# Local attention and a tanh-shrink MLP on one core: a new program with q, k, v cast in one GpSimd ring, bias by TensorE and a new planner

## The chip, the cores and the metric

The kernel runs on one core of a Trainium2 chip. The core has five engines, each with its own queue of instructions worked off in order: TensorE (PE: matmuls, with PEld its weight loads), VectorE (DVE), ScalarE (ACT), GpSimd (POOL) and SyncE (SP). Sixteen DMA engines move data between HBM and the on-chip memory SBUF; SP and POOL issue the transfers here. Matmul results go to PSUM, eight banks of 2 KB per partition. The metric is device time in microseconds of one execution, as the median of several runs.

## The reference

Sliding-window attention with eight global keys and a bias linear in distance, then a two-matrix MLP whose activation is `h - tanh(h)`:

```
q, k, v: (4, 8, 768, 64) f32    n_global, n_local = 8, 96    w_in: (512, 2048)  w_out: (2048, 512)

scores = q @ k.T / 8
rel = pos[:, None] - pos[None, :]
is_global = pos[None, :] < n_global
is_local = (rel >= 0) & (rel < n_local)
dist = where(is_global & ~is_local, n_local, abs(rel))
scores = where(is_global | is_local, scores - slopes * dist, -1e9)    # slopes = 2 ** -(h + 1)
a = softmax(scores)
x = (a @ v).transpose(0, 2, 1, 3).reshape(3072, 512)
h = x @ w_in
out = (h - tanh(h)) @ w_out                                           # (3072, 512) f32
```

## The kernel before

**Tiles.** The 4 x 768 positions are cut into 24 tiles of 128 (`NU`), six per batch (`NQ`), each with all eight heads. Because the window is 96 wide, a tile's queries need only two key blocks: the tile's own (`o = 0`) and the one before it (`o = 1`). The eight global keys and values are copied into the first columns of each previous block (`a_K`, `a_V`). The first tile of a batch has one block only.

**Stages of a tile `u`.** Three loads of 256 KB in f32 from SP (L143), each of 1,024 rows of 256 B; three casts to BF16, on POOL apart from q and k of tile 0 (L157, L160); a transpose of q and k, by PE for `u < 8` (`PE_T`, L169) with its eviction on ACT and DVE (L180, L182), else by a DMA transpose (L173); scores by PE, block by block (`a_S`, L190), each into a pair of PSUM banks; `exp` on ACT (L198); a multiply by a precomputed `exp(-slope * dist)` on DVE (`a_M`, L202); values by PE with a column of ones for the denominator (`a_AV`, L213, L217); the division on DVE (`a_R`, L225, L226); a transpose of x, by PE for `u < 9` (`PE_X`, L240, L249), else by DMA (L252).

**MLP.** The first product runs for one tile at a time for the first six tiles (`EARLY`) and for three together from there on (moving operands of 128 or 384 columns), 16 blocks of 128 hidden units with four matmuls each (`m1`, L273); `tanh` on ACT (L284) and the subtraction on DVE (L290) make g. The second product has 16 matmuls of 512 columns per tile (`m2`, L300), is copied out by ACT (L307) and stored by SP (L310).

**Loads and their order.** POOL issues the eight weight loads of 1 MB each, which are cast on the way (L149, L152). The list `before` gives the order: tiles 0 to 3, four of `w_in`, four of `w_out`, tiles 4 to 6, then the rest. From the third item on, an item after or among the weights waits for the landing of the item two places back (`gate_of`, `started`), so that two are in flight.

**Order on the engines.** All is written out by hand: `plan()` gives each operation an engine, a duration, what it comes after and which buffers it takes, and repeatedly picks the operation that can start first; the resulting list is the order on every queue (`manual_schedule`). `WARM = (1.4, 19.0)` fills PE's gaps up to 19 us of planned time with matmuls on zeros (L265). PSUM is two pools: two pairs of banks (`ps_big`) for scores and values, four single banks (`ps_one`) for the rest. The masks are made with iota on POOL, seven DVE operations on f32 and eight `exp` of 384 columns on ACT (L88 to L107).

Of the kernel before, what the change touches and what calls it, by code (L numbers as in the profile page):

```python
# [1 line left out]

# [10 lines left out]
ENG = mybir.EngineType  # L13


@with_exitstack
def kernel(
# [29 lines left out]
    NV = 8  # L47
    PE_T, PE_X = 8, 9
    HT = 3


    EARLY, EARLY2 = 6, 4
    groups = [[u] for u in range(EARLY)] + [[u, u + 1, u + 2] for u in range(EARLY, NU, HT)]
    group_of = {u: g for g, us in enumerate(groups) for u in us}

    cpool = ctx.enter_context(tc.tile_pool(name="const", bufs=1))
    stpool = ctx.enter_context(tc.tile_pool(name="stage", bufs=4))
    bpool = ctx.enter_context(tc.tile_pool(name="bpool", bufs=3))
    kpool = ctx.enter_context(tc.tile_pool(name="kpool", bufs=9))
    ppool = ctx.enter_context(tc.tile_pool(name="ppool", bufs=3))  # L60
    xpool = ctx.enter_context(tc.tile_pool(name="xpool", bufs=3))
    tpool = ctx.enter_context(tc.tile_pool(name="tpool", bufs=4))
    hpool = ctx.enter_context(tc.tile_pool(name="hpool", bufs=3))
    gpool = ctx.enter_context(tc.tile_pool(name="gpool", bufs=3))
    opool = ctx.enter_context(tc.tile_pool(name="opool", bufs=4))

    ps_big = ctx.enter_context(tc.tile_pool(name="ps_big", bufs=2, space=bass.MemoryType.PSUM))
    ps_one = ctx.enter_context(tc.tile_pool(name="ps_one", bufs=4, space=bass.MemoryType.PSUM))

    ident = cpool.tile([P, P], BF16, name="ident")  # L70
    mk = cpool.tile([P, H, 3, P], BF16, name="mk")
    rmat = cpool.tile([P, 3, P], FP32, name="rmat")
    tmp01 = cpool.tile([P, 2, 2, P], FP32, name="tmp01")
    zero = cpool.tile([P, 512], BF16, name="zero")
    w_in_bf = [cpool.tile([P, CD, DFF // WJ], BF16, name=f"w_in_bf{j}") for j in range(WJ)]
    w_out_bf = [cpool.tile([P, FJ, DM], BF16, name=f"w_out_bf{j}") for j in range(WJ)]
    vb = [cpool.tile([P, H, Dh + 1], BF16, name=f"vb{i}") for i in range(NV)]


    def slot(h):  # L80
        return (h % 2) * NP + h // 2


    def build_masks():


        r = rmat[:, 1:3, :]
        nc.gpsimd.iota(  # L88
            r, pattern=[[P, 2], [1, P]], base=0, channel_multiplier=-1,
            allow_small_or_imprecise_dtypes=True,  # L90
        )
        nc.vector.tensor_scalar(
            out=tmp01[:, 0], in0=r, scalar1=0.0, scalar2=BIG, op0=ALU.is_lt, op1=ALU.mult
        )
        nc.vector.tensor_scalar(
            out=tmp01[:, 1], in0=r, scalar1=float(L), scalar2=BIG, op0=ALU.is_ge, op1=ALU.mult
        )
        nc.vector.tensor_tensor(out=r, in0=r, in1=tmp01[:, 0], op=ALU.max)
        nc.vector.tensor_tensor(out=r, in0=r, in1=tmp01[:, 1], op=ALU.max)
        nc.vector.tensor_copy(out=rmat[:, 0, :], in_=rmat[:, 1, :])  # L100
        nc.vector.tensor_scalar(
            out=rmat[0:G, 0, :], in0=rmat[0:G, 0, :], scalar1=float(L), scalar2=None, op0=ALU.min
        )
        nc.vector.memset(rmat[0:G, 2, :], float(L))
        for h in range(H):
            slope = 2.0 ** (-8.0 * (h + 1) / H)
            nc.scalar.activation(mk[:, slot(h), :, :], rmat, AF.Exp, bias=0.0, scale=-slope)  # L107


    ops = {}  # L110
    w_in_r = moe_w_in.rearrange("(c p) f -> p c f", p=P)
    w_out_r = moe_w_out.rearrange("(c p) d -> p c d", p=P)
    PE, ACT, DVE, POOL, SP = ENG.PE, ENG.Activation, ENG.DVE, ENG.Pool, ENG.SP

    LAT = {PE: 0.17, ACT: 0.1, DVE: 0.1, POOL: 0.12, SP: 0.0}

    def op(key, eng, us, fn, after=(), take=(), give=(), pri=0, dma=0.0):
        ops[key] = dict(
            key=key, eng=eng, us=us, fn=fn, after=[a for a in after if a is not None],
            take=list(take), give=list(give), pri=pri, dma=dma,  # L120
        )

    gate_of = {}
    dmas = {}

    def started(key, i):
        dmas[key] = i
        g = gate_of.get(key)
        if g is not None:
            tc.add_manual_dep(  # L130
                i.ins, dmas[g].ins.name,
                mybir.DependencyInfo(mybir.DependencyClass.Sync, mybir.DependencyReason.DATA),
                reason="order of loads",
            )


    kf, qf, vf = {}, {}, {}
    kq = {}

    def load(u, nm, src, dst):  # L140
        b, i = u // NQ, u % NQ
        dst[u] = stpool.tile([P, H, Dh], FP32, name=nm)
        started(("ld", nm, u), nc.sync.dma_start(  # L143
            out=dst[u], in_=src[b, :, i * P : (i + 1) * P, :].rearrange("h p d -> p h d")
        ))

    def load_w_in(j):
        w = DFF // WJ
        started(("in", j), nc.gpsimd.dma_start(out=w_in_bf[j], in_=w_in_r[:, :, j * w : (j + 1) * w]))  # L149

    def load_w_out(j):
        started(("out", j), nc.gpsimd.dma_start(out=w_out_bf[j], in_=w_out_r[:, j * FJ : (j + 1) * FJ, :]))  # L152

    def cast(u, j, src, eng):
        if u not in kq:
            kq[u] = bpool.tile([P, 2, H * Dh], BF16, name="kq")
        eng.tensor_copy(out=kq[u][:, j, :], in_=src.pop(u).rearrange("p h d -> p (h d)"))  # L157

    def cast_v(u):
        nc.gpsimd.tensor_copy(out=vb[u % NV][:, :, 0:Dh], in_=vf.pop(u))  # L160


    tr, qk, sc, pr, av, xs, xT = {}, {}, {}, {}, {}, {}, {}

    def a_T(u):
        tr[u] = ps_one.tile([P, 2, NP, P], BF16, name="one")
        for j in (1, 0):
            for p in range(NP):
                nc.tensor.transpose(tr[u][:, j, p, :], kq[u][:, j, p * P : (p + 1) * P], ident)  # L169

    def a_DT(u):
        qk[u] = kpool.tile([P, 2, NP, P], BF16, name="qk")
        nc.sync.dma_start_transpose(  # L173
            out=qk[u].rearrange("p a b f -> p (a b) f"), in_=kq.pop(u).rearrange("p a f -> p (a f)")
        )

    def a_Te(u, j):
        if j == 1:
            qk[u] = kpool.tile([P, 2, NP, P], BF16, name="qk")
            nc.scalar.copy(out=qk[u][:, 1], in_=tr[u][:, 1])  # L180
        else:
            nc.vector.tensor_copy(out=qk[u][:, 0], in_=tr[u][:, 0])  # L182

    def a_S(u, o):
        sc[u, o] = ps_big.tile([P, 2, 512], FP32, name="big")
        s = sc[u, o].rearrange("q a (h f) -> q (a h) f", f=P)
        for p in range(NP):
            for hh in range(2):
                r = slice(hh * Dh, (hh + 1) * Dh)
                nc.tensor.matmul(  # L190
                    s[:, slot(2 * p + hh), :], qk[u - o][r, 1, p, :], qk[u][r, 0, p, :],
                    start=True, stop=True,
                )

    def a_E(u, o):
        pr[u, o] = ppool.tile([P, H, P], BF16, name="po" if o else "pd")
        s = sc.pop((u, o)).rearrange("q a (h f) -> q (a h) f", f=P)
        nc.scalar.activation(pr[u, o], s, AF.Exp, bias=0.0, scale=scale)  # L198

    def a_M(u, o):  # L200
        m = 2 if o else min(u % NQ, 1)
        nc.vector.tensor_tensor(out=pr[u, o], in0=pr[u, o], in1=mk[:, :, m, :], op=ALU.mult)  # L202

    def a_K(u):
        nc.vector.tensor_copy(out=qk[u][:, 1, :, 0:G], in_=qk[u - u % NQ][:, 1, :, 0:G])

    def a_AV(u):
        av[u] = ps_big.tile([P, 2, 512], FP32, name="big")
        t = av[u][:, :, 0 : (H // 2) * (Dh + 1)].rearrange("q a (h d) -> q a h d", d=Dh + 1)
        last = u % NQ == 0  # L210
        for h in range(H):
            dst = t[:, h // (H // 2), h % (H // 2), :]
            nc.tensor.matmul(  # L213
                dst, pr[u, 0][:, slot(h), :], vb[u % NV][:, h, :], start=True, stop=last,
            )
            if not last:
                nc.tensor.matmul(  # L217
                    dst, pr[u, 1][:, slot(h), :], vb[(u - 1) % NV][:, h, :], start=False, stop=True,
                )

    def a_R(u):
        xs[u] = xpool.tile([P, H, Dh], BF16, name="x")
        t = av.pop(u)[:, :, 0 : (H // 2) * (Dh + 1)].rearrange("q a (h d) -> q a h d", d=Dh + 1)
        rden = xpool.tile([P, 2, H // 2, 1], FP32, name="rden")
        nc.vector.reciprocal(rden, t[:, :, :, Dh : Dh + 1])  # L225
# [5 lines left out]
    def a_V(u):  # L231
        nc.vector.tensor_copy(
            out=vb[u % NV][0:G, :, 0:Dh], in_=vb[(u - u % NQ) % NV][0:G, :, 0:Dh]
        )
# [321 lines left out]
```

## Time and profile before

| what | value |
| --- | --- |
| three runs | 227.22, 226.76, 227.09 us; median 227.09 |
| span of the profiled execution, first to last instruction | 224.4 us |
| granted TensorE clock | 1.000 |
| last second-product matmul group ends, last copy starts | 220.8 us |
| HBM read, written | 27.26 MB, 6.29 MB |
| hardware queue (SP's transfers) | 103,392 packets, 31.34 MB, 72.3% of 16 engines' span |
| software ring (POOL's transfers) | 4,224 packets, 4.19 MB, 12.1% |
| first-product matmuls, 384 columns | 384, mean 326 ns |
| second-product matmuls, 512 columns | 384, mean 379 ns |

The time of the profiled execution itself isn't given, so the span is compared with the median of the runs: 2.7 us lie around it. A mean duration of a matmul overlaps the next one's; the pace of a run of matmuls is read from their starts. A group's idle time is that of its engine just before its instructions, with what ended it; on an engine that isn't the bottleneck it costs nothing.

### The profile page before, as it was taken

The numbers are of one execution on the slowest core, as the hardware profiler recorded it, in microseconds if no ns is written. First come the engines' busy times: TensorE is split into PE (matmuls) and PEld (weight loads), VectorE is DVE, ScalarE is ACT, GpSimd is POOL, SyncE is SP. The second block draws the span as 40 slices with busy tenths as digits, with TensorE's granted clock in tenths as the row PEclk, the third lists the DMA queues.
The fourth block names the chain that finished last, engine by engine and source line by source line (L and its number), as shares of the span: only waits on it lengthen the run. The fifth ranks groups of instructions, "written<-read, shape, count | busy, mean of one in ns | idle before, by whom it ended". The sixth has DMA issues, their size and how long they took to land.

```text
span 224.4 us, 5020 instructions
## 1 busy us (share of the span) xinstructions
PE 211.9 (94%) x1975; PEld 126.0 (56%) x1998; DVE 136.4 (61%) x279; ACT 124.2 (55%) x205; POOL 53.8 (24%) x85
## 2 busy tenths in 40 slices
PE   6898899999899999899999999999999999999993
PEld 2455897555785565445555555555555555555541
DVE  5367785215898599743897767677675743444300
ACT  5655654256775487543778384746664644544321
POOL 1473212064463432233233332322000000000000
PEclk9999999999999999999999999999999999999999
DMA  7999999999999999999999999997514121011112
GB/s 151 219 207 152 151 191 164 221 204 290 240 190 201 189 265 194 193 200 196 250 240 198 206 187 234 223 170 150 120 33 107 50 70 47 3 48 47 47 49 95
DMA packets 107640, 35.85 MB, mean 160 GB/s; under 512 B 100448, under 2 KB 104544, under 8 KB 107616
## 3 DMA queue, kind: packets, MB, share of 16 engines
q1 hardware_dynamic: 103392, 31.34, 72.3%
q0 software_dynamic: 4224, 4.19, 12.1%
q8 instruction: 15, 0.25, 0.5%
q14 instruction: 9, 0.07, 0.1%
HBM read 27.26 MB, written 6.29 MB: 150 GB/s over the span
## 4 chain that ended last, share of the span: by engine, by line
PE 78%; DMA 7%; SPq 6%; DVE 3%; ACT 3%; issue 1%
PE one L273 35%; PE one L300 34%; SPq L143 5%; PE big L190 4%; DMA w_in_bf_97<-in_moe_w_in_dram 3%; DMA vf<-in_v_dram 3%; PE big L213 2%; PE big L217 2%; DMA xT<-x 2%; ACT pd L198 2%; DVE po L202 1%; DVE pd L202 1%; PE one L240 1%; PE one L169 1%; DVE xT L249 1%
## 5 line engine op out<-in xcount | busy, mean ns | idle before, releaser
L284 ACT ACTIVATE th<-one 128x384 f32<-128x384 f32 (+1 forms) x120 | 60.7, 516 | 51.7 <-PE one L273 47.7
L290 DVE TENSOR_TENSOR g<-one,th 128x384 bf16<-128x384 f32 (+1 forms) x120 | 67.6, 579 | 32.7 <-ACT th L284 30.7
L300 PEld LDWEIGHTS <-g 128*128 128x128 bf16 x384 | 36.0, 98 | 36.0
L198 ACT ACTIVATE pd<-big 128x1024 bf16<-128x1024 f32 x24 | 24.6, 1024 | 16.6 <-PE big L190 14.9
L157 POOL CAST kq<-kf 128x512 bf16<-128x512 f32 x23 | 14.8, 645 | 56.7 <-DMA kf<-in_k_dram 46.6
L307 ACT COPY ot<-one 128x512 f32<-128x512 f32 x24 | 14.1, 587 | 23.9 <-PE one L300 23.8
L202 DVE TENSOR_TENSOR pd<-pd,mk 128x1024 bf16<-128x1024 bf16 x24 | 18.4, 768 | 11.9 <-ACT pd L198 11.5
L273 PE MATMUL one<-xT,w_in_bf_96 128*128 128x128 bf16 (+1 forms) x192 | 24.6, 273 | 1.1 <-DVE xT L249 0.9
L273 PE MATMUL one<-xT,w_in_bf_97 128*128 128x128 bf16 (+1 forms) x192 | 24.7, 273 | 0.8 <-DMA w_in_bf_97<-in_moe_w_in_dram 0.8
L273 PE MATMUL one<-xT,w_in_bf_99 128*128 128x128 bf16 (+1 forms) x192 | 25.2, 273 | 0.0
L273 PE MATMUL one<-xT,w_in_bf_98 128*128 128x128 bf16 (+1 forms) x192 | 25.1, 273 | 0.0
L300 PE MATMUL one<-w_out_bf_100,g 128*128 128x512 bf16 x88 | 24.1, 379 | 0.5 <-issue 0.2
L300 PE MATMUL one<-w_out_bf_103,g 128*128 128x512 bf16 x94 | 24.1, 379 | 0.2
L300 PE MATMUL one<-w_out_bf_101,g 128*128 128x512 bf16 x92 | 23.8, 379 | 0.2
L300 PE MATMUL one<-w_out_bf_102,g 128*128 128x512 bf16 x89 | 23.1, 379 | 0.4 <-issue 0.2
L198 ACT ACTIVATE po<-big 128x1024 bf16<-128x1024 f32 x20 | 20.5, 1025 | 1.4 <-PE big L190 1.4
L273 PEld LDWEIGHTS <-w_in_bf_96 128*128 128x128 bf16 x192 | 14.6, 98 | 9.1 <-issue 1.3
L273 PEld LDWEIGHTS <-w_in_bf_99 128*128 128x128 bf16 x192 | 14.8, 98 | 7.4
L273 PEld LDWEIGHTS <-w_in_bf_97 128*128 128x128 bf16 x192 | 14.4, 98 | 7.9 <-DMA w_in_bf_97<-in_moe_w_in_dram 1.0
L273 PEld LDWEIGHTS <-w_in_bf_98 128*128 128x128 bf16 x192 | 14.6, 98 | 7.2
L157 POOL CAST kq<-qf 128x512 bf16<-128x512 f32 x23 | 15.6, 678 | 10.0 <-DMA qf<-in_q_dram 9.9
L202 DVE TENSOR_TENSOR po<-po,mk 128x1024 bf16<-128x1024 bf16 x20 | 15.9, 797 | 3.0 <-ACT po L198 3.0
(91 smaller groups left out, 181.2 us busy)
## 6 DMA issues: line engine op xcount, KB each, us to landing
kf<-in_k_dram SPq DMA_DIRECT2D x24, 256.0 KB, 4.0
qf<-in_q_dram SPq DMA_DIRECT2D x24, 256.0 KB, 4.4
vf<-in_v_dram SPq DMA_DIRECT2D x24, 256.0 KB, 4.8
out_dram<-ot SPq DMA_DIRECT2D x24, 256.0 KB, 2.9
w_in_bf_96<-in_moe_w_in_dram POOLq DMA_DIRECT2D x1, 512.0 KB, 6.4
w_in_bf_97<-in_moe_w_in_dram POOLq DMA_DIRECT2D x1, 512.0 KB, 6.5
w_in_bf_98<-in_moe_w_in_dram POOLq DMA_DIRECT2D x1, 512.0 KB, 6.6
w_in_bf_99<-in_moe_w_in_dram POOLq DMA_DIRECT2D x1, 512.0 KB, 5.3
```

The costliest lines, as they stand in the source:

```text
L143: started(("ld", nm, u), nc.sync.dma_start(out=dst[u], in_=src[b, :, i * P : (i + 1) * P, :].rearrange("h p d -> p h d")))
L157: eng.tensor_copy(out=kq[u][:, j, :], in_=src.pop(u).rearrange("p h d -> p (h d)"))
L190: nc.tensor.matmul(s[:, slot(2 * p + hh), :], qk[u - o][r, 1, p, :], qk[u][r, 0, p, :], start=True, stop=True,)
L198: nc.scalar.activation(pr[u, o], s, AF.Exp, bias=0.0, scale=scale)
L202: nc.vector.tensor_tensor(out=pr[u, o], in0=pr[u, o], in1=mk[:, :, m, :], op=ALU.mult)
L213: nc.tensor.matmul(dst, pr[u, 0][:, slot(h), :], vb[u % NV][:, h, :], start=True, stop=last,)
L217: nc.tensor.matmul(dst, pr[u, 1][:, slot(h), :], vb[(u - 1) % NV][:, h, :], start=False, stop=True,)
L273: nc.tensor.matmul(t[:, (f - f0) * n : (f - f0 + 1) * n], w_in_bf[j][:, c, fo : fo + P], xT[b][:, c, o : o + n], start=(c == 0), stop=(c = ...
L284: nc.scalar.activation(h_view(ths[g, f0], g), h_view(hs[g, f0], g), AF.Tanh, bias=0.0, scale=1.0)
L290: nc.vector.tensor_tensor(out=gs[b][:, f0 : f0 + m, o : o + n], in0=h_view(hs.pop((g, f0)), g), in1=h_view(ths.pop((g, f0)), g), op=ALU.su ...
L300: nc.tensor.matmul(os_[u], gs[u // HT][:, f, t * P : (t + 1) * P], w_out_bf[f // FJ][:, f % FJ, :], start=(f == 0), stop=(f == CF - 1),)
L307: nc.scalar.copy(out=ots[u], in_=os_.pop(u))
```

## The change

The program is written anew around the same tiles and the same arithmetic.

- **Loads.** SP loads only q and k of tiles 0 and 1, in f32, as 1 KB rows (four positions of a head are contiguous in HBM); DVE and ACT cast them. All else goes through POOL's one ring, cast to BF16 on the way: q and k of tiles 2 and 3 in 1 KB rows, the other q, k and all v in 256 B rows straight into their BF16 buffers. POOL's casts are gone, and so are the gates between loads; the order is that of the list `ring`.
- **Transposes.** In the four row tiles, a partition holds four positions of two heads, and the evictions put the columns back in order; tiles 2 and 3 take 16 transposes instead of 8. PE transposes q, k for `u < 6` and x for `u < 6`; the rest are DMA transposes from SP. The two transposed halves lie in two banks.
- **Bias.** `dist` (one 128 x 128 block for each kind of mask) and scaled diagonal `slopes` are made in BF16 on POOL and DVE. For tiles 0 to 2 PE adds `dist` times `slopes` into the scores' banks before the scores, and there is no multiply. For later tiles PE makes the masks by the same product and ACT takes their `exp`.
- **Scores.** Both blocks of a tile run together, in four banks.
- **MLP.** One tile at a time for the first four tiles, two together from there on (256 columns, two hidden blocks a unit). The last tile's output is made in pieces of 256, 128 and 128 columns, each copied and stored by itself. POOL issues all stores but those of the last two tiles. Evictions may go to ACT or DVE.
- **Planner.** A simulation of events with all eight banks in one pool, two DMA rings that share the engines, and priorities by tile; warm matmuls end at 11 us of planned time.

```diff
-    PE_T, PE_X = 8, 9
-    HT = 3
-    EARLY, EARLY2 = 6, 4
-    groups = [[u] for u in range(EARLY)] + [[u, u + 1, u + 2] for u in range(EARLY, NU, HT)]
+    ROWS = 4
+    HW = 2
+    PE_T = 6
+    PE_X = 6
+    BIASED = 3
+    SINGLE = 4
+    NK, NV, NQK = 5, 10, 8
+    groups = [[u] for u in range(SINGLE)] + [[u, u + 1] for u in range(SINGLE, NU, 2)]
...
+    WARM = (1.3, 11.0)
+    plan.pool("bank", 8, {7: WARM[1]})
+    buffers("kq", NK, [P, 2, H * Dh], BF16)
+    buffers("ot", 4, [P, DM], FP32)
...
+    def bias(holder, o, m, stop):
+        for a in range(2):
+            nc.tensor.matmul(
+                bank(holder, 2 * o + a), dist[:, m, :], slopes[:, a * NP : (a + 1) * NP, :], start=True, stop=stop
+            )
...
+    def load_rows(e, holder, dst, src, u):
+        s = rows_of(src, u).rearrange("(a b) (g r) d -> g a b (r d)", b=2, r=R4)
+        eng(e).dma_start(out=dst, in_=s)
+
+    def load_natural(e, dst, src, u):
+        eng(e).dma_start(out=dst, in_=rows_of(src, u).rearrange("h p d -> p h d"))
...
     def a_T(u):
+        s = buf(("kq", u))
         for j in (1, 0):
+            t = bank(("tr", u, j)).bitcast(BF16)[:, 0 : NP * P].rearrange("q (p f) -> q p f", p=NP)
             for p in range(NP):
-                nc.tensor.transpose(tr[u][:, j, p, :], kq[u][:, j, p * P : (p + 1) * P], ident)
+                if HW <= u < ROWS:
+                    for hh in range(2):
+                        c = hh * R4 * Dh + p * Dh
+                        nc.tensor.transpose(t[hh * Dh : (hh + 1) * Dh, p, :], s[:, j, c : c + Dh], ident)
+                else:
+                    nc.tensor.transpose(t[:, p, :], s[:, j, p * P : (p + 1) * P], ident)
+
+    def a_Te(e, u, j):
+        t = bank(("tr", u, j)).bitcast(BF16)[:, 0 : NP * P]
+        d = buf(("qk", u))[:, j]
+        if u < ROWS:
+            copy(e, d.rearrange("q p (g r) -> q r g p", r=R4), t.rearrange("q (r g p) -> q r g p", r=R4, p=NP))
+        else:
+            copy(e, d, t.rearrange("q (p f) -> q p f", p=NP))
...
+    def a_S(u):
+        for o in blocks(u):
+            for p in range(NP):
+                for hh in range(2):
+                    r = slice(hh * Dh, (hh + 1) * Dh)
+                    nc.tensor.matmul(
+                        bank(("s", u), 2 * o + hh)[:, p * P : (p + 1) * P], buf(("qk", u - o))[r, 1, p, :],
+                        buf(("qk", u))[r, 0, p, :], start=u >= BIASED, stop=u >= BIASED or p == NP - 1,
+                    )
...
+    ring = [("v", 0), ("v", 1)]
+    for u in range(HW, ROWS):
+        ring += [("kq", u), ("v", u)]
+    ring += [("in", j) for j in range(WJ)] + [("kq", 4), ("v", 4), ("out", 0), ("out", 1), ("kq", 5), ("v", 5)]
+    ring += [("out", 2), ("out", 3)]
+    ring += [x for u in range(ROWS, NU) for x in (("kq", u), ("v", u)) if x not in ring]
...
+        cols = [(0, DM)] if u < NU - 1 else [(0, 256), (256, 384), (384, 512)]
...
+            se = POOL if u < NU - 2 else SP
```

## The prediction

> **What bounds the kernel now.** I read the page's busy shares and 40 slices first, then the chain that ended last, then a table of stages, then the groups with their shapes kept apart.
>
> ```profile
> PE 211.9 (94%) x1975; PEld 126.0 (56%) x1998; DVE 136.4 (61%) x279; ACT 124.2 (55%) x205; POOL 53.8 (24%) x85
> ...
> DMA  7999999999999999999999999997514121011112
> ```
>
> TensorE (PE) is the bound on average, but the second line says that the DMA engines are full for the first 27 slices of 5.6 us, to about 155 us. Only PE and DMA can set the end. The stages show how PE's 94% is spread:
>
> ```profile
> 0.00:8.00 8.00, 5.98 (x25) 2.48 (x26) 3.68 (x19) 5.17 (x10) 1.96 (x9) 1.00 0.94 172
> 8.00:21.00 13.00, 11.27 (x135) 6.73 (x136) 8.07 (x18) 6.76 (x8) 7.61 (x12) 1.00 1.18 186
> 21.00:25.00 4.00, 3.21 (x63) 2.77 (x60) 3.40 (x8) 3.15 (x4) 0.35 (x2) 1.00 1.22 195
> 25.00:47.00 22.00, 21.89 (x288) 17.27 (x288) 11.52 (x19) 9.56 (x17) 4.92 (x7) 1.00 1.06 178
> 47.00:70.00 23.00, 21.48 (x319) 15.90 (x318) 16.73 (x33) 14.39 (x21) 11.07 (x16) 1.00 1.14 232
> 70.00:130.00 60.00, 57.92 (x526) 32.30 (x528) 44.41 (x89) 37.33 (x61) 19.57 (x30) 1.00 1.16 215
> 130.00:213.00 83.00, 82.42 (x605) 45.22 (x615) 48.63 (x95) 46.07 (x83) 8.27 (x12) 1.00 0.50 100
> ```
>
> Columns: stretch, length, then PE, PEld, DVE, ACT and POOL busy, granted clock, DMA share, GB/s. From 47 us on PE idles 1.5 + 2.1 + 0.6 = 4.2 us; nothing much is to be had there. The front is poor although it looks busy, because it is filled with matmuls on zeros:
>
> ```profile
> L265 PE MATMUL one<-zero 128*128 128x512 bf16 x40 | 11.5, 425 | 1.4 <-DVE zero L514 1.2 <-issue 0.2
> ```
>
> What ends last there is loads, in the chain by time (start, length, what):
>
> ```profile
> 12.18 5.71 DMA vf<-in_v_dram
> 17.89 0.30 issue
> 18.19 6.52 DMA w_in_bf_97<-in_moe_w_in_dram
> 24.75 2.85 PE one L273 x48
> ```
>
> So twelve q, k, v loads and then the weights set when PE has real work. The change is worth what it moves **there**, provided the DMA engines keep ahead later.
>
> **PE's work.** Prices are start-to-start in the chain: 16 matmuls of 128 columns in 0.89 us (55.6 ns), 4 of 384 in 0.65 (162.5 ns), 4 of 512 in 0.86 (216 ns). For 256 columns the line through the first two gives 109 ns. First product: before 6 x 64 x 55.6 ns + 6 x 64 x 162.5 ns = 83.8 us; after 4 x 64 x 55.6 + 10 x 64 x 109 = 84.0, +0.2. Second product: 384 x 216 ns = 82.9 both; cutting the last tile in three adds 0.1. Transposes of q, k: 8 x 0.45 before (8 in 0.45); after 4 x 0.45 + 2 x 0.9, since tiles 2 and 3 take 16 instead of 8: 0. Transposes of x: 9 x 0.33 to 6 x 0.33, -1.0. Scores: 16 in one run take 0.55 us, two runs of 8 take 2 x 0.33, so 0.11 for each pair now split; about half of 20 are split, -1.0. Bias: 5 blocks and 3 masks, 2 matmuls of 512 each, 16 x 216 ns = +3.5. Net +1.8 us, nearly all in the front.
>
> **The front, new.** DMA prices: weights are issued 3.0 to 3.3 us apart, each released by a landing, so 3.13 us per 1 MB. A 256 KB load with 256 B rows is issued by SP every 1.19 us (1.14 and the gap) with the engines full. A load in 1 KB rows has no row here; by bytes it is 3.13/4 = 0.78, by its twin 1.19. I take 0.78, because its rows are nearer in size to the weights' 2 KB. The price that matters, 256 B rows cast in the GpSimd ring, has no row either. Below: by bytes 0.78. Above: by rows, 1024 against a weight's 512, 6.3. I take 1.2, the hardware queue's load with the same rows and bytes. POOL's issue: 512 rows took 0.74, SP's 1024 rows 1.14; bounds 0.74 to 1.5, taken 1.0.
>
> k of tile 0 lands at about 3.6 instead of 4.0, q, k, q follow 0.78 apart, to 6. The eight mask exponentials (3.4 us) leave ACT's head, which in the old profile held tile 0's eviction until 7.07. Strided evictions of the row tiles cost between 0.42 (the contiguous row) and 1.0; 0.55 taken; DVE and ACT have the room (both under 65% busy to 21 us). Constants by near rows (0.2 to 0.35 each) end by 4 us on DVE and 2.2 on POOL, so v of tile 0 is issued near 3.9 and lands near 8. x of tile 0 is ready at about 10 instead of 12.9. The ring then carries v1, k2, q2, v2, k3, q3, v3: about 5 x 1.2 + 4 x 0.78 with its share beside SP, to 14.3, and 3.13 per weight: the first lands near 18.3 (now 20.6), then 21.5, 24.6, 27.7. Tile 4 (3.6) and two w_out: 34.5, 37.6; tile 5, and the last two: 44.4, 47.5. In the old kernel the last lands at 42.5 (POOL issue at 36.9 plus 5.6). **The weights end later**, but tiles 4 and 5 are among them; now they land at 45 to 49.
>
> PE: all of the first product of tiles 0 to 3 (14.2 us) is done by 31.3. It lacks work for 1.6 us before 34.5, and for 1.9 before 44.4 (tile 4's and tile 5's attention fill the rest). By 47.9 three quarters of the second product of four tiles is done.
>
> **Sum.** In the old run 220.8 - 47.0 - 4.2 idle = 169.6 us of work remain at 47.0. At 47.9 the new one has, against that: first product +0.5 (260 of its small matmuls were done, now 256, and the +0.2); second product 48 matmuls done against 40, -1.7; attention 18 tiles x 1.03 + 0.8 left against 20 x 1.05 + 4 x 0.45 + 5 x 0.33, -5.0; joined scores -0.5. So 162.9 us. With the same 4.2 idle PE ends at 47.9 + 162.9 + 4.2 = 215.0. The tail: the last eviction is of 128 columns (0.3 instead of 0.59), the store then as before, 3.2 after PE instead of 3.6. Span 218.2. The old span is 224.4 and the median of the runs shown 227.1; with the same 2.7 around it: **221 us**.
>
> **Costed at nothing, and their cover.** POOL's 46 casts of k and q and 24 of v go: POOL is off the chain. DVE's multiplies, mean 768 and 797 ns against a least of 678, should shorten without them: DVE is at 61%. After the change POOL issues three loads and a store per tile, 3 x 1.0 + 0.4 to 0.74, at most 5.2 by the upper bound, inside PE's 8.1 per tile (3.49 + 3.46 + 0.55 + 0.48 and 0.1 of switches); without that cover each excess microsecond delays the ring. A store on POOL waits for its eviction, and behind it stand the loads of later tiles; a load waits for one of 5 kq buffers, and behind it stand stores. Five tiles of lead and four ot buffers (some 30 us) hide both. SP keeps only transposes: one waiting for its q and k holds back the x transposes behind it; SP loses 1.14 x 3 of issues per tile.
>
> Rows first: POOL took 0.74 to 0.88 us for each weight while DVE ran, so no lock shows. The Trainium skill, "SBUF — State Buffer", § Who interferes with whom, speaks against the change: DVE copies in a two-port mode lock GpSimd out of the port with which it writes descriptors. By it POOL would wait at most for the two small copies per tile (0.16 + 0.29), 5.7 of 8.1 us: the sum is unchanged by either.
>
> The granted clock is 1.00 in every stage, with warm matmuls to 19 us and no PE wait over 1.2; they now end at 11. The skill, "TensorE: Matmul & The Clock Gate", § Part 1, drops the clock to half after an idle window of about 3.4 us; no gap of my sum is so long, and if one were, some 1.7 us of work would be lost.
>
> **Rivals.**
>
> *DMA becomes the bound (slower, 0.22).* Place: loads of tiles 6 to 23 in the ring. SP issued k of successive tiles at 102.1 and 108.6, and at 140.0 and 146.2, so a tile took the full engines 6.2 to 6.5 us; with transposes counted I take 6.85 at 1.2 per load. Each 0.1 adds 0.3 per tile; at 1.63 the DMA needs 8.1, as PE does. Price at 1.8: the front ends 6 later, 53.5 + 18 x 8.65 = 209, less 4 of trailing transposes, plus 26 for the last pair (two DMA transposes of about 4, attention 4.5, products 14) and 6 for store and surroundings: 237. At 2.0 about 245. For it: a ring packet takes long (12.1% of 16 engines for 4,224 packets is 103 ns, for 2 KB). Against: twice the bytes per time of the 256 B loads.
>
> *A hand order that doesn't fit (slower or level, 0.13).* PE runs in the written order, and two score blocks hold four of eight banks at once. If each of 20 pairs stalls a product by 0.6 us for a bank or a late load, +12: 233; at 0.3, 227. Against: by the rows' durations a tile holds banks for 4 x 1.7 + 2 x 1.0 (scores), 2 x 1.5 (values), 4 x 2.5 (first product) and 9 (output), 31 of 8 x 8.1 = 65 bank-microseconds; old waits on PE after 25 us sum to 3.4.
>
> *Gain lost (same, 0.05).* Ring loads at 1.55: ten of them in the front give 3.5 back, the later starvation 2.5: 227.
>
> *Weights faster (faster, 0.15).* The weights no longer wait for landings two back. At 2.6 us each the front ends 4 earlier: 217.
>
> **Chances.** Forecast 0.45, with its own range 217 to 225; faster weights 0.15; same 0.05; slower 0.35. No change means within 0.2%, about what this measurement can tell. The range 214 to 236 leaves out the DMA rival's upper half and little below.
>
> **What would show it.** Right: warm matmuls end near 11, first w_in matmul near 18, last w_out landing near 47, PE idle under 6 us after 48, the DMA slices full to about 165. Wrong: DMA slices full past 195 with PE waiting for qk or xT; ring loads landing over 1.6 us apart; PE waits on ACT or DVE releases of ps repeated in every tile.

## The result and the profile after

The changed kernel takes 249.98 us (median of 4 runs, 247.47 to 250.82); the kernel before took 226.93 us beside it. The ratio is 1.102, 95% interval [1.096, 1.109]: slower by a tenth, where 221 us were forecast. Here and below a time is the median of all runs, while a ratio leaves out slow runs, those more than 1.5% above the kernel's fastest, so differences between kernels are read from the ratios (0.01 is about 2.3 us). The profiled execution has a span of 247.4 us.

The page's busy shares, and its slices of TensorE clock and of DMA (6.2 us each):

```profile
PE 215.8 (87%) x2133; PEld 146.4 (59%) x2133; DVE 134.1 (54%) x253; ACT 126.8 (51%) x177; POOL 79.1 (32%) x105
...
PEclk9998779999999999999999999999999999999999
DMA  6999999910169799939989969989943240120202
```

PE's busy time rose by 3.9 us (with 6.3 us fewer matmuls on zeros), but its share fell from 94% to 87%: PE waits more. Two things are new in the slices. The clock falls in slices 4 to 6 (it is halved from 17.5 to 20.9 and from 27.7 to 34.6 us), and the DMA engines, in the kernel before full without a break to 155 us, stand nearly still in slices 9 to 11 (50 to 68 us). The table of stages, with the stretches and columns of the prediction's, says where PE loses:

```profile
8.00:21.00 13.00, 7.80 (x75) 4.00 (x73) 10.04 (x9) 8.24 (x6) 8.72 (x11) 0.87 1.47 196
21.00:25.00 4.00, 1.78 (x48) 1.46 (x47) 2.03 (x3) 2.06 (x2) 1.57 (x2) 1.00 1.84 178
25.00:47.00 22.00, 17.70 (x276) 16.92 (x276) 13.04 (x26) 14.61 (x21) 9.55 (x12) 0.84 1.87 176
47.00:70.00 23.00, 20.65 (x199) 12.29 (x198) 8.40 (x16) 9.68 (x15) 1.67 (x3) 1.00 0.25 55
70.00:130.00 60.00, 52.69 (x514) 35.09 (x513) 34.68 (x64) 30.91 (x45) 25.71 (x32) 1.00 1.36 126
130.00:213.00 83.00, 77.22 (x768) 52.26 (x767) 51.51 (x99) 43.39 (x63) 22.47 (x29) 1.00 1.05 107
```

There are two losses. **In the front**, from 8 to 47 us, PE is busy 27.3 of 39 us, part of that at a low clock; before it was 36.4, some of it matmuls on zeros. **Later**, from 47 to 213 us, it idles 2.4 + 7.3 + 5.8 = 15.4 us, where it idled 4.2 before.

The chain that ended last, by time (start, length, what), shows what the front waits for:

```profile
10.82 4.71 DVE qk L265 x2
15.53 0.04 issue
15.57 0.29 PE ps L407 x4
15.86 0.60 PE ps L381 x16
16.48 0.04 issue
16.52 0.22 DVE rden L415
16.74 0.02 issue
16.76 0.69 DVE x L416
17.45 2.41 DVE qk L265 x2
```

In the kernel before, loads stood in this part of the chain. Now it is the evictions of the transposed q and k (L265 on DVE, L263 on ACT). Their groups (count, busy us, mean ns, idle before them) are:

```profile
L263 ACT COPY qk<-ps 128x512 bf16<-128x512 bf16 x7 | 11.1, 1736 | 4.5 <-PE ps L349 3.4
L265 DVE COPY qk<-ps 128x512 bf16<-128x512 bf16 x5 | 9.9, 2059 | 1.8 <-PE ps L351 1.8
```

These groups hold two sorts: the eight evictions of the row tiles 0 to 3 take about 2.4 us each, the four of tiles 4 and 5 about 0.6. The same copy without a stride took 0.42 (DVE) to 0.58 us (ACT) before:

```profile
L180 ACT COPY qk<-one 128x512 bf16<-128x512 bf16 x8 | 4.7, 583 | 1.1 <-PE one L169 1.1
L182 DVE COPY qk<-one 128x512 bf16<-128x512 bf16 x8 | 3.4, 424 | 9.2 <-ACT qk L180 9.2
```

The first w_in matmul comes at 29.97 us, where 18 was forecast and 21.44 measured before, although the first weight lands at 16.1, earlier than forecast. What is late is x, not the weight.

The later loss is spread. PE's own waits after 66 us are small, and four of these five are of a kind that the kernel before had little of (engine, line, what it waited for; us in all, times, longest):

```profile
PE ps L381 <- DMA qk<-kq: 4.2, 4, 1.6
...
PE ps L448 <- ACT pr L388: 2.5, 3, 1.2
PE ps L473 <- ACT pr L388: 2.2, 2, 1.1
PE ps L473 <- DVE x L416: 2.0, 2, 1.0
PE ps L448 <- DVE x L416: 1.5, 3, 1.1
```

A product (L448, L473) reads neither the scores' exponentials (`pr`) nor x of the tile in attention, and yet waits for the instructions that make them. One place in the timeline, tile 9, shows it from both ends (start, length, engine, line; in brackets the idle time before it and its releaser):

```profile
95.13 1.02 ACT L388 ACTIVATE pr<-ps 128x1024 bf16<-128x1024 f32 x1 [0.54 <-PE ps L381]
...
96.12 1.04 PE L448 MATMUL ps<-xT,w_in_bf 128*128 128x256 bf16 x8
...
97.19 1.02 ACT L388 ACTIVATE pr<-ps 128x1024 bf16<-128x1024 f32 x1 [1.04 <-PE ps L448]
...
98.27 0.93 PE L448 MATMUL ps<-xT,w_in_bf 128*128 128x256 bf16 x7 [1.11 <-ACT pr L388]
```

The second `exp` of tile 9 should follow the first at 96.15. It starts when a product's matmuls end, and the next product starts when this `exp` ends. In the plan tile 9's scores hold banks 0, 1, 2 and 6; the second `exp` reads banks 2 and 6 as one access with a stride. The product before it lies in bank 3, the one after it in bank 4. Both are disjoint from 2 and 6, but lie **between** them. Of the plan's 71 pairs of banks that one instruction reads, 45 are not neighbours.

A third suspect is GpSimd, which from 42.35 to 66.02 us issues nothing: a store waits for its eviction, and the loads stand behind it.

### The profile page after: what moved, and what is told of

It reads as the page before. It is cut to its first block, busy times and chain, and to the rows that moved or that the text cites. A ratio compares the mean times of both kernels' runs of the same rounds, so it can differ in the third digit from the quotient of the medians.

```text
span 247.4 us, 5185 instructions
## 1 busy us (share of the span) xinstructions
PE 215.8 (87%) x2133; PEld 146.4 (59%) x2133; DVE 134.1 (54%) x253; ACT 126.8 (51%) x177; POOL 79.1 (32%) x105
## 4 chain that ended last, share of the span: by engine, by line
PE 65%; DMA 15%; DVE 10%; ACT 6%; issue 2%; POOL 1%; DVEq 0%; ACTq 0%
PE ps L473 28%; PE ps L448 26%; DMA qk<-kq 13%; ACT pr L388 4%; PE ps L381 4%; DVE qk L265 4%; PE ps L407 4%; DVE x L416 3%; DMA kq<-in_k_dram 2%; PE ps L685 2%; DVE rden L415 1%; PE ps L310 1%; ACT qk L263 1%; PE ps L351 1%; DVE g L464 1%
## 5 line engine op out<-in xcount | busy, mean ns | idle before, releaser
L448 PE MATMUL ps<-xT,w_in_bf 128*128 128x256 bf16 (+1 forms) x896 | 95.2, 261 | 6.4 <-ACT pr L388 3.6
L473 PE MATMUL ps<-w_out_bf,g 128*128 128x512 bf16 (+2 forms) x416 | 92.6, 363 | 5.6 <-DVE x L416 2.4
L448 PEld LDWEIGHTS <-w_in_bf 128*128 128x128 bf16 x896 | 78.0, 100 | 21.6 <-issue 8.4
L464 DVE TENSOR_TENSOR g<-ps,th 128x512 bf16<-128x512 f32 x96 | 64.3, 685 | 35.6 <-ACT th L458 33.5
L458 ACT ACTIVATE th<-ps 128x512 f32<-128x512 f32 x96 | 56.3, 599 | 42.3 <-PE ps L448 31.8
L473 PEld LDWEIGHTS <-g 128*128 128x128 bf16 x416 | 37.3, 98 | 40.9 <-issue 7.3
L388 ACT ACTIVATE pr<-ps 128x1024 bf16<-128x1024 f32 x44 | 43.6, 1029 | 30.5 <-PE ps L381 15.0
L392 DVE TENSOR_TENSOR pr<-pr,mk 128x1024 bf16<-128x1024 bf16 x39 | 26.6, 689 | 23.4 <-ACT pr L388 23.4
L263 ACT COPY ot<-ps 128x512 f32<-128x512 f32 (+2 forms) x21 | 11.4, 544 | 33.8 <-PE ps L473 33.8
L332 POOL DMA_DIRECT2D vb<-in_v_dram x24 | 21.9, 914 | 3.0 <-DMA w_in_bf<-in_moe_w_in_dram 1.6
L332 POOL DMA_DIRECT2D kq<-in_q_dram x20 | 18.1, 906 | 5.7 <-PE ps L427 2.7
L332 POOL DMA_DIRECT2D kq<-in_k_dram x20 | 18.2, 910 | 4.7 <-PE ps L427 2.1
L263 ACT COPY qk<-ps 128x512 bf16<-128x512 bf16 x7 | 11.1, 1736 | 4.5 <-PE ps L349 3.4
L265 DVE COPY qk<-ps 128x512 bf16<-128x512 bf16 x5 | 9.9, 2059 | 1.8 <-PE ps L351 1.8
L265 DVE COPY qk<-qk 128x32 bf16<-128x32 bf16 x16 | 3.5, 218 | 10.5 <-PE ps L381 10.5
```

What stands on the lines that cost most here:

```text
L263: nc.scalar.copy(out=out, in_=in_)
L265: eng(e).tensor_copy(out=out, in_=in_)
L332: eng(e).dma_start(out=dst, in_=rows_of(src, u).rearrange("h p d -> p h d"))
L388: nc.scalar.activation(d, banks(("s", u), 2 * o, 2 * o + 1), AF.Exp, bias=0.0, scale=scale)
L392: nc.vector.tensor_tensor(out=t, in0=t, in1=mk[:, mask_of(u, o)], op=ALU.mult)
L448: nc.tensor.matmul(t[:, (f - f0) * n : (f - f0 + 1) * n], w_in_bf[j][:, c, fo : fo + P], x[:, c, 0:n], start=(c == 0), stop=(c == CD - 1),)
```

## The experiments

Three theories, not exclusive. **A**: the strided evictions are the front's loss. **B**: accesses over a gap between banks are ordered against the banks in the gap, and that is the later loss. **C**: waiting stores on GpSimd hold back loads. Each kernel below computes the whole reference, and all ratios are to the kernel before. "Both repairs" is A's and B's repair together.

**A alone.** The copy walks its columns in the order of the destination, so that it reads PSUM with a stride of 256 B and writes SBUF contiguously, instead of the reverse. The plan and its order are the same.

```diff
-copy(e, d.rearrange("q p (g r) -> q r g p", r=R4), t.rearrange("q (r g p) -> q r g p", r=R4, p=NP))
+copy(e, d.rearrange("q p (g r) -> q p g r", r=R4), t.rearrange("q (r g p) -> q p g r", r=R4, p=NP))
```

> Edit: the eight evictions of the row tiles walk their copy in the destination's order, so they write without gaps and read PSUM with a stride; nothing else is changed. Theory A (the writes of two bytes 256 bytes apart cost the 2.35 us each, and they hold the front): the eight take 0.4 to 0.7 us, the first matmul with w_in moves from 30.0 to about 18 to 20 us, the granted clock between 10 and 40 us returns to about 1, and the time falls by 8 to 12 us, to 238 to 242. Rival (the stride costs as much on the reading side, or the front waits for something else, such as the ring): evictions stay near 2.4 us, or they shorten and the first w_in matmul stays past 27; time above 246.

239.36 us, ratio 1.050 [1.044, 1.057]. The groups of the same evictions:

```profile
L263 ACT COPY qk<-ps 128x512 bf16<-128x512 bf16 x7 | 3.8, 587 | 1.6 <-PE ps L349 1.0 <-PE ps L351 0.5
L265 DVE COPY qk<-ps 128x512 bf16<-128x512 bf16 x5 | 3.1, 630 | 0.0
```

It is the side that is written which costs: 2.4 us with the stride on the BF16 side in SBUF, 0.6 with it on the PSUM side. The first w_in matmul moves from 29.97 to 19.8 us, all as theory A expected, but the clock is not whole yet (0.71 from 21 to 25 us). The false waits of the later part stay: L448 and L473 on `pr` wait 2.5 and 2.2 us as before.

**B alone.** The planner gives out pairs of neighbouring banks only.

```diff
+    def pick(self, have, p, n, now):
...
+        free = {i: (t, i) for t, i in have if t <= now + 1e-9}
+        if n == 1:
+            return [min(free.values(), key=lambda g: (g[1] ^ 1 in free, g))] if free else []
+        pairs = sorted((max(free[i], free[i + 1]), i) for i in range(0, 8, 2) if i in free and i + 1 in free)
+        return [free[j] for _, i in pairs[: n // 2] for j in (i, i + 1)]
...
```

> Edit: the planner hands out banks for scores, values and masks only as neighbouring pairs, and single banks preferably from broken pairs; evictions as in the changed kernel. Theory B (an access to two banks that are not neighbours is ordered against work in the banks between them, so exp and the division wait for first- and second-product matmuls and PE then waits for them): waits of exp on w_in or w_out matmuls (about 8 us) and PE's waits for exp and the division (about 13 us in all) vanish nearly, PE idle after 66 us falls from 13 to 3 to 5 us, time 238 to 242. Rival (eight banks are too few, or the loads come late): PE idle after 66 us stays 10 to 15 us, time 246 to 252.

236.81 us, ratio 1.033 [1.025, 1.042], a little better than theory B's 238 to 242. The waits after 60 us on scores and `exp`:

```profile
ACT pr L407 <- PE ps L400: 9.3, 8, 2.6
...
PE ps L400 <- DMA qk<-kq: 3.3, 4, 1.5
```

`exp` waits for its own scores only, and of PE's waits that for a transposed q or k is the one left above 0.6 us. The front is as bad as it was: evictions of 1.8 to 2.0 us in the mean, the first w_in matmul at 30.2.

**Both repairs.**

> Both edits. If A and B hold and are separate places, the gains add: 226 to 232. If one theory fails, the time is that of the other edit alone. If they mask one another (a faster front only meets the later waits), less than the sum: 232 to 238.

221.29 us, ratio 0.972 [0.967, 0.976]: faster than before. Its stages, in the same stretches:

```profile
8.00:21.00 13.00, 11.51 (x201) 8.44 (x202) 8.31 (x21) 9.68 (x13) 8.60 (x11) 1.00 1.47 196
21.00:25.00 4.00, 4.00 (x83) 4.00 (x81) 3.61 (x8) 2.70 (x6) 0.89 (x2) 1.00 1.84 182
25.00:47.00 22.00, 21.84 (x287) 16.16 (x288) 13.59 (x25) 11.68 (x18) 10.26 (x12) 1.00 1.83 176
47.00:70.00 23.00, 22.31 (x199) 14.63 (x198) 11.96 (x23) 13.22 (x20) 10.97 (x15) 1.00 1.28 157
70.00:130.00 60.00, 56.96 (x590) 40.25 (x597) 41.37 (x78) 33.91 (x50) 28.41 (x35) 1.00 1.58 141
130.00:213.00 83.00, 78.68 (x691) 53.57 (x701) 46.78 (x82) 40.56 (x61) 12.64 (x18) 1.00 0.66 82
```

The front is full, the clock whole, the first w_in matmul comes at 17.65, and the DMA engines are busy in the stage where they stood still, 47 to 70 us (1.28 against 0.25). A's repair alone makes it 0.90 and B's 0.42, so that pause followed mostly from the late front. Of the ratio of 1.102, A's repair alone takes 0.052 (some 12 us), B's 0.069 (16), both 0.131 (30): the gains add, to a little more than their sum, and the time lies below the 226 to 232 that were expected of it.

**C.** Both repairs, with all stores issued by SP.

```diff
-            se = POOL if u < NU - 2 else SP
+            se = SP
```

> Both edits, and all stores are issued by SP, so that POOL issues loads alone. Theory C (a store on POOL that waits for its eviction holds the loads behind it, they then come in bursts and collide with the DMA transposes, whose landings took up to 9.7 us): PE's waits for qk (4.2 us) vanish and the time is 3 to 6 us under the run with both edits. Rival (loads have five tiles of lead, so a held load costs nothing; or stores on SP hold the transposes instead): within 1.5 us of it, or slower.

221.70 us, ratio 0.975 [0.970, 0.981]: no gain. The wait has changed place: SP's stores now wait, and its transposes stand behind them. PE has a hole at 66 to 72 us (2.3 of 6 us busy), and the granted clock is 0.50 from 70 to 77 us. So SP is no better place for the stores; that a store which waits on POOL costs nothing isn't shown by this, since the new place has a cost of its own.

**B turned round.** Both repairs, and the same plan and order, but each pair of neighbours is renamed to two banks four apart. If B is wrong, nothing changes.

```diff
+        x, y = x // 2 + 4 * (x % 2), y // 2 + 4 * (y % 2)
...
-        return ps[:, holds[holder][a], :]
+        x = holds[holder][a]
+        return ps[:, x // 2 + 4 * (x % 2), :]
```

> The version with both edits, same plan, same order on every engine, same lifetimes of banks; only the position of each bank is renamed when the code is written, so that a pair which was neighbours (0,1), (2,3) ... becomes (0,4), (1,5), (2,6), (3,7), with three other banks between. Theory B (an access over a gap is ordered against the banks inside the gap) says that waits of exp on product matmuls and PE's waits for exp and the division come back, 13 us or more, as each pair now spans three other banks: 234 to 248. Rival (the gain of the adjacent version came from the changed order and the changed lifetimes of the banks): within 2 us of the version with both edits, 219 to 223.

253.57 us, ratio 1.121 [1.112, 1.129]: over 30 us for names of banks, more than the expected range, as all 71 pairs now have a gap instead of 45. The false waits are back and longer (after 60 us):

```profile
ACT pr L409 <- PE ps L494: 15.0, 9, 3.7
...
PE ps L469 <- ACT pr L409: 5.7, 9, 1.2
PE ps L494 <- ACT pr L409: 5.5, 8, 1.1
```

That isolates B: order and number of banks are the same, and so are the durations of the instructions (`exp` takes 1.02 us in both).

**Without 1 KB rows.** B's repair, and q and k of all tiles in 256 B rows; the strided evictions go with the rows.

```diff
-    ROWS = 4
+    ROWS = 0
...
```

> Adjacent pairs, and no 1 KB rows: q and k of tiles 0 to 3 come in 256 B rows like all others (tiles 0 and 1 still in f32 from SP), with plain casts, 8 transposes and plain evictions. Against the version with both edits this leaves out the rows alone. If the rows are worth what bytes say (0.78 against 1.2 us for eight loads), the first w_in matmul comes 2 to 3.5 us later and the time is 223 to 225; if the rows' costs (twice the transposes in two tiles, strided evictions) eat it, within 1 us of 221.3.

229.76 us, ratio 0.998 [0.993, 1.004]. The version with the rows, with evictions that cost 0.6, is some 6 us faster (0.998 against 0.972), more than expected. The first w_in matmul comes 2.0 us later here (19.7), within what bytes said; whether the other 4 us are the rows' or those of the other order that the planner makes without them, isn't shown.

**Without the bias by TensorE.** Both repairs; the masks of tiles 0 to 2 are multiplied in by DVE, like the others.

```diff
-    BIASED = 3
+    BIASED = 0
```

> Both edits, and no bias by PE for tiles 0 to 2: they get the multiply by the mask on DVE like all others; PE still makes the three masks. PE loses 10 matmuls of 216 ns (2.2 us) where it has gaps anyway, DVE gets five multiplies of 0.69 (3.5 us) on the way of tiles 0 to 2. If the front is set by the weights' landing (17.6), within 1 us; if by the attention chain of the first tiles, 1 to 3 us slower; if by PE's work, up to 2 us faster.

225.46 us, ratio 0.989 [0.984, 0.994]: the version with the bias in the scores' banks is some 4 us faster. But this isn't the front's gain: without the bias the first w_in matmul comes no later (17.0 against 17.65). The run without it has a hole at 50 to 66 us (12.8 of 16 us busy, clock 0.79), where PE waits for DVE's multiply or for x with no product to fill, so the 4 us may be the other order's throughout; what the bias itself is worth stays open.

**The planner told of slow evictions.** B's repair with the strided writes left in; the plan counts 2.4 us for each of the eight, and warm matmuls run to 24 us of planned time.

```diff
-    WARM = (1.3, 11.0)
+    WARM = (1.3, 24.0)
...
+            c = 2.4 if u < ROWS else 0.6
...
```

> Adjacent pairs with the strided writes left in, but the planner is told 2.4 us for the eight slow evictions, and warm matmuls go on to 24 us of planned time. Theory A says the evictions themselves hold the front (9.6 us on each of two engines), so this regains only what the lower clock and the wrong order cost: first w_in matmul at 24 to 29, clock above 0.95 in 10 to 40 us, time 230 to 235 against 236.8. Rival (the lateness comes from the order that was made for the wrong price, or from the clock): 222 to 227.

229.05 us, ratio 1.004 [0.999, 1.010]. The evictions are as slow (2.07 and 1.67 us in the mean of the groups), yet the ratio falls by 0.029 against B alone (1.033), some 7 us; the first w_in matmul comes at 19.2, long before the 24 that theory A expected, and the clock is 1.00 throughout.

**The same order with quick evictions.** The last run's plan, with A's edit.

> The order made for slow evictions (2.4 us in the planner, warm matmuls to 24 us of planned time, neighbouring bank pairs) with the evictions writing contiguously, so that they take 0.6 us. If the slow evictions themselves still cost something in the run with the same order (ratio 1.004), this goes below it, to between 0.97 and 0.985, as the run with both repairs did. Rival, that the planned order alone costs the front: the ratio stays within 0.005 of 1.004, though the evictions are short.

229.00 us, ratio 1.006 [1.002, 1.010]: the expected gain is missed and the rival holds. So the evictions' 1.8 us apiece costs some 14 us under an order made for 0.6 (1.033 against 0.972) and nothing under one made for 2.4. This order has a price of its own, some 8 us over both repairs (1.006 against 0.972). The traces suggest where it lies. These are the matmuls on zeros here and with both repairs:

```profile
L705 PE MATMUL ps<-zero 128*128 128x512 bf16 x50 | 13.5, 404 | 1.2 <-DVE vb L325 1.2
L704 PE MATMUL ps<-zero 128*128 128x512 bf16 x14 | 5.0, 485 | 1.2 <-DVE vb L325 1.2
```

PE in all is busy 214.1 and 205.7 us, so the difference is about that of the filler. That it stands in front of real work fits, but no run changes the filler alone.

**The later part, after both repairs.** Three kernels go on from there. First the plan counts more for DMA transposes, +2.5 us for q and k and +1.0 for x:

```diff
-               pri=base, ring=SP, work=W_DT, lag=D_LAG, tail=D_TAIL)
+               pri=base, ring=SP, work=W_DT, lag=D_LAG, tail=D_TAIL + 2.5)
...
```

> Both repairs, and the planner counts 2.5 us more for a DMA transpose of q and k and 1.0 us more for one of x. If PE's four waits for a transposed q or k (5.5 us in all with both repairs) are on the path that sets the end, they vanish from PE's waits and the time falls from 221.3 to between 216 and 220. Rival, that DMA sets the pace there: the waits move to the casting loads or to x and the time stays at 221 plus or minus 2.

221.78 us, ratio 0.976 [0.970, 0.982]. PE's waits for transposed q and k (5.5 us with both repairs) are gone, but no time is gained. PE's rows between 64 and 74 us, and the clock by 2 us, say where it went:

```profile
66.42 0.39 PE L400 MATMUL ps<-qk,qk 64*128 64x128 bf16 x8
68.44 0.20 PE L426 MATMUL ps<-vb,pr 128*128 128x65 bf16 x1 [1.62 <-DVE pr L411]
69.35 1.01 PE L426 MATMUL ps<-vb,pr 128*128 128x65 bf16 x15 [0.71 <-DVE pr L411]
71.60 2.72 PE L467 MATMUL ps<-xT,w_in_bf 128*128 128x256 bf16 x12 [1.24 <-DMA xT<-x]
```

```profile
66.00:70.00 4.00, 1.66 (x38) 1.33 (x35) 2.56 (x6) 2.34 (x3) 3.31 (x5) 0.89 0.53 111
70.00:72.00 2.00, 0.76 (x10) 0.53 (x8) 1.36 (x3) 0.00 (x0) 2.00 (x3) 0.50 1.80 131
72.00:74.00 2.00, 2.00 (x11) 1.45 (x10) 0.00 (x0) 0.45 (x1) 2.00 (x3) 0.50 1.79 165
74.00:76.00 2.00, 2.00 (x12) 1.43 (x11) 0.79 (x2) 0.75 (x2) 1.02 (x2) 0.52 2.24 156
```

A tile's attention runs with no product left to fill PE: 3.6 us of idle time, and then, as an estimate, 2.3 us of work lost to the halved clock (0.76 x 0.5 + 2.0 x 0.5 + 2.0 x 0.48).

Then the stores of this kernel from ACT (`se = ACT` for all but the last two tiles):

> As the last run, with the stores issued by ScalarE, which mostly makes the evictions that they wait for, instead of GpSimd. If waiting stores hold back GpSimd's loads at a net cost, the loads are issued evenly, no GpSimd wait on an output tile is left and the time is 2 to 4 us below that of the last run. Rival, that the lead of the loads covers it: within 1.5 us of the last run; ScalarE's own work is some 55% of the span, so the issues cost it little.

223.02 us, ratio 0.982 [0.977, 0.987]: within 1.5 us of the last run, as the rival said. Neither place for the stores is better than POOL.

Last, the measured prices of the ring in the plan (`W_NAT, W_WT = 0.9, 2.6` instead of 1.2 and 3.14) with the longer transposes:

> Both repairs and the longer transposes, and the planner is told what the ring's loads measured: 0.9 us for a 256 KB load and 2.6 us for a weight, instead of 1.2 and 3.14. If the order made for too slow a ring left time in the front, the first w_in matmul comes near 16 instead of 17.6 and the time falls to 215 to 219. Rival, that loads which come early in any case find their work early in any order: within 2 us of the run with the longer transposes alone.

220.90 us, ratio 0.971 [0.964, 0.977]. The first w_in matmul comes at 16.5, 1.1 earlier, but the end is where it was: PE waits 6.6 us for transposed q and k here. The first and the third are not told from both repairs (0.972 [0.967, 0.976]) by their intervals; the stores from ACT lie just above it.

## Why the prediction was wrong, step by step

**The step that failed first: "Strided evictions of the row tiles cost between 0.42 ... and 1.0; 0.55 taken".** They took 2.40 us, four times the value and more than twice the upper bound. The bound was a guess: the trace before had no copy that wrote its elements singly at a distance, and no row of it supports 1.0. The cover named for them (DVE and ACT under 65% busy to 21 us) was no cover in this order, because x of four tiles goes through them one after another, and the order on every queue had been made for short ones. A's repair alone gives back some 12 us; on top of B's it is worth 14.

**The second: the rival of the hand order named the wrong mechanism.** It counted banks, 31 of 65 bank-microseconds, and priced stalls for want of one. At the place shown the product had its bank, and with neighbouring pairs the same eight banks were enough. What cost was which banks: a pair with a gap was ordered against the banks in it. The sign to look for was right ("PE waits on ACT or DVE releases of ps"), but its +12 us is too little: the run with this fault alone is some 18 us over both repairs (1.050 against 0.972). It was set at 0.13, and no case of the prediction had two faults at once, so none held 250.

**The clock step failed.** The sum took the granted clock as 1.00, since no gap came near 3.4 us. In the changed kernel, the table of 2 us stretches shows:

```profile
24.00:26.00 2.00, 0.65 (x14) 0.46 (x9) 1.59 (x5) 2.00 (x2) 1.70 (x3) 1.00 2.12 171
26.00:28.00 2.00, 0.26 (x1) 0.10 (x1) 0.34 (x1) 2.00 (x2) 1.18 (x2) 0.93 1.24 207
28.00:30.00 2.00, 1.15 (x16) 0.77 (x16) 0.17 (x1) 2.00 (x3) 0.96 (x2) 0.50 1.25 204
30.00:32.00 2.00, 2.00 (x24) 2.00 (x24) 0.69 (x1) 0.32 (x1) 0.61 (x2) 0.50 2.08 167
32.00:34.00 2.00, 2.00 (x28) 2.00 (x26) 0.11 (x1) 1.02 (x1) 1.79 (x3) 0.50 1.90 181
```

Busy time by the part of the clock that was missing gives, as an estimate, 2.9 us of work lost here (24 to 36 us) and 1.3 at 16 to 22. No PE wait in these stretches was longer than 2 us. The Trainium skill, "TensorE: Matmul & The Clock Gate", § Part 1, ties the halved clock to an idle window of about 3.4 us; here PE worked 0.9 of the 4 us from 24 to 28 and the clock halved all the same. So a stretch with little work was enough here, without one unbroken gap, and the prediction looked only for a gap. How little is not settled: in the 3.4 us before the fall at 27.7 us PE was busy for 0.41 us, in those before the fall at 17.5 for 1.77.

**Right, and hidden by these.** With both repairs the first w_in matmul comes at 17.65 ("near 18") and the time is 221.29 (221). That agreement is partly luck. The four w_in weights landed 2.4 us apart in the mean (17.6 to 24.7) instead of 3.13, 256 KB loads took about 0.85 us instead of 1.2, and the last w_out landed at 40.4 instead of 47.5, which is the case of faster weights, priced at 217. (The old trace held such gaps too: landings at 24.71 and 27.24, 36.63 and 39.17.) From 47 us to its end PE is busy 161.6 us, where the sum has 162.9 at 47.9, or 163.8 at 47: some 2 us ahead. Against that it idled 8.0 us from 47 to 213 us (0.7 + 3.0 + 4.3) instead of 4.2, much of it waiting for transposed q and k (5.5 us in all). Two errors of opposite sign nearly cancel. The transposed x of tile 0 was ready at 13.6 instead of 10, which costs nothing while the first weight lands at 17.6. In the sum itself the attention terms differ by 5.1, not 5.0, and the old first weight landed at 20.3, not 20.6; neither matters.

**The DMA rival fell.** What it needed was not there: the ring is faster than taken, and the last quarter of the DMA slices is mostly empty. What is left of it with both repairs is the 5.5 us that PE waits for transposed q and k.

**POOL's waiting stores.** The five tiles' lead did not cover 23.7 us of waiting in the changed kernel; the loads stopped. But this came mostly from the late front, and with both repairs moving the stores to SP or ACT gained nothing. Whether they cost nothing in the kernel the sum described isn't shown, as SP at least had waits of its own.

**PE's work.** +1.8 us was forecast; busy time rose by 3.9, which contains the low clock and fewer matmuls on zeros (5.2 us against 11.5). With both repairs, where the clock is whole, PE is busy 200.7 us without those on zeros, 200.4 before: no more than forecast, as far as busy time tells. The bias was costed as +3.5 us of PE work and nothing in return; the run without it is 4 us slower, but for a hole that its order has, so this neither confirms the price nor shows a return.

**Still open.** How much of the 14 us under the wrong order is the waits and how much the clock was not tried apart. By an estimate the clock is at most some 6: with B's repair alone it was halved for two stretches of 6.8 us, in which PE was busy 5.84 and 6.25 us. Nor was the order for slow evictions tried without its filler, or the filler alone.

## What to carry to other kernels

A copy like this one, which permutes BF16 columns on the way out of PSUM, should write contiguously and take its stride on the PSUM side (0.6 against 2.4 us), and an operation whose layout no row of the trace has needs a run by itself before an order is built on it. Where one instruction reads two PSUM banks, give it neighbours: in this program the access was ordered against the banks between. In a program ordered by hand, a wrong price costs not its own excess but what the order does with it: 14.4 us of excess (eight evictions, 1.8 each) cost some 14 us in one order and nothing in another.

## What was not expected of the hardware

- A 128 x 512 BF16 copy from PSUM that writes SBUF with elements 256 B apart takes 2.4 us on DVE and on ACT, 4.7 ns for each of 512 columns; reading with that stride and writing contiguously takes 0.58 to 0.63 us, against 0.42 to 0.60 without a stride.
- Reading two banks with a gap as one access made instructions on the banks between wait, on PE, ACT and DVE (up to 15.0 us in all for one kind of wait, with every pair apart). Whether a tracker of the program or the chip imposes it, these runs do not say.
- The ring that casts was faster than the hardware queue's rows suggested: 0.85 us for 1,024 rows of 256 B, and 0.87 to 0.96 us of GpSimd to issue them (both repairs).
- The granted clock halved after 3.4 us in which PE was busy 0.41 us (changed kernel, 24.3 to 27.7) or 1.32 (longer transposes, 65.7 to 69.1), with no wait above 2 us. It stayed at half for 3.4 or 6.8 us each time. Nine of the thirteen traces from the changed kernel on show such a fall before the tail.
